# Decay products of an RWKV-7 block from its first token: inverse taken token-major, k and b scaled in place and then turned

## The chip, the cores and the metric

One core of one Trainium2 chip. The metric is device time in microseconds (us) of one launch, the median of three runs. The engines are named as in the profile: PE (TensorE), DVE (VectorE), ACT (ScalarE), POOL (GpSimd), SP (the queue that issues most transfers).

## The reference

A recurrent attention block is followed by a feed-forward layer. Batch 4, 8 heads, 768 tokens, 40 features a head; then 3072 rows of 320 go through 320 x 2048 and 2048 x 320 with a hard-swish between.

```python
# r, k, v, w, a, b: (4, 8, 768, 40); state: (4, 8, 40, 40)
for t in range(S):
    y[:, :, t] = einsum('bhd,bhde->bhe', rt, state)
    Sa = einsum('bhde,bhe->bhd', state, at)
    state = state * wt[:, :, None, :] - einsum('bhd,bhe->bhde', Sa, bt) \
            + einsum('bhd,bhe->bhde', vt, kt)
x = y.transpose(0, 2, 1, 3).reshape(3072, 320)
h = x @ w_in
out = (h * clip(h + 3.0, 0.0, 6.0) / 6.0) @ w_out
```

w lies between 0.85 and 0.95, and the two weight matrices arrive as 64-bit floats.

## The kernel before

The recurrence is cut into 24 **units**: unit i holds 64 tokens of 8 heads of two batch rows, so 128 rows of 320 values. Each group of 4 units covers the same 64 or the next 64 tokens of all four batch rows. Gamma is the running product of w inside a unit; a, k, b and the result are scaled by gamma or by its inverse, so that the recurrence over 64 tokens becomes matrix products and the inverse of a triangular 64 x 64 matrix for each head (called "inversion" below: a long series of small DVE operations for 4 units together, `prod` and `x` in the profile).

"Turning" is PE's transpose of a tile from token-major (tokens on partitions) to feature-major (features of two heads on partitions):

```python
def turn_pairs(x):                      # 4 transposes of 128 x 128 into one PSUM bank
    o = ps_any([P, NPR, P])             # five banks "any", used in turn
    for n in range(NPR):
        nc.tensor.transpose(out=o[:, n, :], in_=x[:, 2 * n:2 * n + 2, :]..., identity=ident[:])
    return o
```

The preparation of a unit counts gamma from the *middle* of the 64 tokens, backwards and forwards:

```python
def w_stage():
    wt = turn_pairs(o["WN"]); yield PE
    nc.scalar.activation(out=wv[:, :, 0, 1:HB + 1], in_=x[:, :, 0, ::-1], func=AF.Copy)
    nc.scalar.activation(out=wv[:, :, 1, 1:HB + 1], in_=x[:, :, 1, :], func=AF.Copy)
    fetch("W", following(i))
    nc.vector.tensor_tensor_scan(out=prods..., data0=wm[:], data1=start[:], ...)   # 128 x 528
def gam_stage():
    nc.vector.reciprocal(gv[:, :, 0:HB], prods backward half)                      # 128 x 256
    nc.gpsimd.tensor_copy(gv[:, :, HB:BL], ...)
    nc.gpsimd.tensor_copy(rv[:, :, 0:HB], ...)
    nc.gpsimd.tensor_copy(dec..., ...)            # the decay over each half unit
def a_stage():
    x = turn_pairs(o["AN"]); yield PE
    nc.vector.reciprocal(rv[:, :, HB:BL], prods forward half)                      # 128 x 256
    nc.vector.tensor_tensor(out=at[:], in0=x[:], in1=o["G"][:], op=ALU.mult)
def b_stage():                                    # k_stage is the same with K, kt
    x = turn_pairs(o["BN"]); yield PE
    nc.vector.tensor_tensor(out=bt[:], in0=x[:], in1=o["rg"][:], op=ALU.mult)
def factor_stage():                               # token-major k and b, needed later by sn and y
    (4 transposes of o["rg"]); yield PE
    nc.scalar.activation(out=rgt[:], in_=..., func=AF.Copy)
    t = grp.tile([P, HD + WPAD], F32, name="KBt", tag="KBt", bufs=NU + 2)
    nc.gpsimd.memset(t[:, 2 * HD:], 0.0)
    for name in "KB": nc.gpsimd.tensor_tensor(out=o[name]..., in0=o[name + "N"]..., in1=rgt[:], op=ALU.mult)
    for name in "BK": fetch(name, following(i))
```

F (at with bt) and E (at with kt) are matrix products of the scaled tiles. F feeds the inversion.

In a unit's own steps the state is scaled at the start and added to later, and the result is scaled at the end:

```python
def s_RT():
    ...
    nc.gpsimd.tensor_tensor(out=scale[:], in0=last_dec[p][:], in1=dec[:, 0], op=ALU.mult)
    nc.gpsimd.tensor_copy(last_dec[p][:], dec[:, 1])
    nc.vector.tensor_tensor(out=st..., in0=st..., in1=scale..., op=ALU.mult)
def s_sn():
    (64 matrix products of K, B with V, U); yield PE
    for q in range(2): nc.vector.tensor_tensor(out=st[:, q, :, 0:D], in0=sn[q], in1=st[:, q, :, 0:D], op=ALU.add)
def s_y():
    ...
    nc.gpsimd.tensor_tensor(out=yg[:], in0=m["ys"]..., in1=o["G"][:], op=ALU.mult)
```

The order of work is fixed in the program. At the start, the 64-bit weights are converted piece by piece (20 pieces, five steps each, lines 299 to 328) beside the preparation of the first group. A second group of four is prepared beside the weights' end. From unit 4 on the kernel is in its **steady part**: each unit takes four steps. In each step PE gets the attention products due in it first (those of the unit itself, and the preparation of a unit five ahead), and then about 3.5 pieces of the feed-forward layer, 6.2 while an inversion runs. Results are collected in a fixed order.

```python
OWN_STAGES   = [["RT", "VT"], ["R", "C", "S"], ["U", "UT", "rS"], ["sn", "H"], ["y"], ["move", "move2"]]
AHEAD_STAGES = [["W", "gam"], ["A", "B"], ["F", "K"], ["E", "factor"], ["EV"]]
CLOSE_STAGES = [["W", "gam"], ["A", "B"], ["F", "K", "factor"], ["E"], ["EV"]]
PRODUCTS = ["RT", "VT", "W", "S", "A", "B", "K", "factor", "y", "EV", "R", "C", "U", "UT", "rS", "sn", "H", "E", "F"]
RESULTS  = ["RT", "y", "W", "gam", "VT", "EV", "R", "S", "C", "A", "B", "move", "move2", "U", "UT", "rS", "F", "K", "sn", "H", "E", "factor"]
```

PRODUCTS is PE's order inside one part of a step, RESULTS that of the operations that empty PE's banks.

Of the kernel before, what the change touches and what calls it, by code (L numbers as in the profile page):

```python
# [8 lines left out]
F32 = mybir.dt.float32  # L9
# [20 lines left out]
def kernel(  # L30
# [52 lines left out]
    WPAD = HD + SLOT - D  # L83
# [74 lines left out]
    def second(name):  # L158

        tag = {"B": "S", "K": "U"}[name]  # L160
        return padded(grp.tile([P, H, SLOT], F32, name=name + "1", tag=tag, bufs=1), name)

# [8 lines left out]
    SCAN = NB * 2 * (HB + 1)  # L171
    start = const.tile([P, SCAN], F32, name="start")
    nc.vector.memset(start[:], 0.0)
    nc.vector.memset(start[:].rearrange("p (n i) -> p n i", i=HB + 1)[:, :, 0:1], 1.0)
    wm = const.tile([P, SCAN], F32, name="wm")
    nc.vector.memset(wm[:], 0.0)
    inputs, others = {}, {}
    for name in "WABK":
        inputs[name] = padded(const.tile([P, H, SLOT], F32, name=name), name)
    seconds()  # L180
    for name in "BK":
        others[name] = second(name)
# [17 lines left out]
    state, last_dec = [], []  # L200
    for p in range(NP):
        t = const.tile([P, 2, NPR, SLOT], F32, name=f"state{p}")
        nc.vector.memset(t[:], 0.0)
        state.append(t)
        t = const.tile([P, 2, NPR], F32, name=f"last{p}")
        nc.vector.memset(t[:], 1.0)
        last_dec.append(t)
# [47 lines left out]
    def load_weights():  # L255
# [24 lines left out]

        while load():
            pass
# [4 lines left out]
        parts = [grp.tile([P, HD + WPAD], F32, name=f"parts{n}", tag="KBt", bufs=NU + 2)  # L287
                 for n in range(2)]
        parts = [t[:, 0:2 * WC].bitcast(U32).rearrange("p (n c) -> p n c", n=2) for t in parts]
        for n in range(PIECES + 1):  # L290
            now = None
            if n < PIECES:
# [3 lines left out]
                hi = raw[:, :, :, 1]  # L296
                x = parts[n % 2]
                now = out, raw, x
# [5 lines left out]
            if before:  # L304
                out, raw, y = before
                m, yf = raw[:, :, :, 1].bitcast(F32), y.bitcast(F32)
# [3 lines left out]
                if len(out.shape) == 4:  # L310
                    m, yf = (z.rearrange("p n (j c) -> p n j c", c=out.shape[3]) for z in (m, yf))
                nc.vector.tensor_tensor(out=out, in0=m, in1=yf, op=ALU.mult)
# [6 lines left out]
            if now:  # L319
                nc.vector.scalar_tensor_tensor(x, hi, 0x80000000, x, ALU.bitwise_and,  # L320
                                               ALU.bitwise_or)
# [64 lines left out]
    def fetch(name, i, engine=None):  # L386
# [5 lines left out]
        if name == "V":  # L392
            t = values[i % AHEAD]
        else:
            t = (others if i < 2 * NU and i % 2 and name != "R" else inputs)[name]
# [55 lines left out]
    def prepare(i, F):  # L451
        n, o = i % NU, data[i]
        def w_stage():
            wt = turn_pairs(o["WN"])
            yield PE

            wv = wm[:].rearrange("p (r m i) -> p r m i", m=2, i=HB + 1)
            x = wt[:].rearrange("p r (q m i) -> p (r q) m i", q=2, m=2)
            nc.scalar.activation(out=wv[:, :, 0, 1:HB + 1], in_=x[:, :, 0, ::-1], func=AF.Copy)
            nc.scalar.activation(out=wv[:, :, 1, 1:HB + 1], in_=x[:, :, 1, :], func=AF.Copy)  # L460
            fetch("W", following(i))
            prods = o["prods"] = tmp.tile([P, NB, 2, HB + 1], F32, name="prods", bufs=2)
            nc.vector.tensor_tensor_scan(  # L463
                out=prods[:].rearrange("p r m i -> p (r m i)"), data0=wm[:], data1=start[:],
                initial=0.0, op0=ALU.mult, op1=ALU.add,
            )

        def gam_stage():

            gam = o["G"] = grp.tile([P, NPR, P], F32, name="gam", tag="gam", bufs=NU + 2)  # L470
            rgam = o["rg"] = tmp.tile([P, NPR, P], F32, name="rgam", bufs=2)
            gv = gam[:].rearrange("p r (q i) -> p (r q) i", q=2)
            rv = rgam[:].rearrange("p r (q i) -> p (r q) i", q=2)
            nc.vector.reciprocal(gv[:, :, 0:HB], o["prods"][:, :, 0, 1:HB + 1][:, :, ::-1])  # L474
            nc.gpsimd.tensor_copy(gv[:, :, HB:BL], o["prods"][:, :, 1, 0:HB])
            nc.gpsimd.tensor_copy(rv[:, :, 0:HB], o["prods"][:, :, 0, 0:HB][:, :, ::-1])
            dec = grp.tile([P, 2, 2, NPR], F32, name="dec", tag="dec", bufs=NU + 2)
            nc.gpsimd.tensor_copy(dec[:].rearrange("p m q r -> p r q m"),
                                  o["prods"][:].rearrange("p (r q) m i -> p r q m i", q=2)[:, :, :, :, HB])
            o["dec"] = dec  # L480
            if i <= 2 * NU:
# [3 lines left out]
        def a_stage():  # L485
            x = turn_pairs(o["AN"])
            yield PE
            rv = o["rg"][:].rearrange("p r (q i) -> p (r q) i", q=2)
            nc.vector.reciprocal(rv[:, :, HB:BL], o["prods"][:, :, 1, 1:HB + 1])  # L489
            at = o["at"] = grp.tile([P, NPR, P], F32, name="at", tag="at")  # L490
            nc.vector.tensor_tensor(out=at[:], in0=x[:], in1=o["G"][:], op=ALU.mult)
            fetch("A", following(i))

        def b_stage():
            x = turn_pairs(o["BN"])
            yield PE
            bt = o["bt"] = turned("bt")
            nc.vector.tensor_tensor(out=bt[:], in0=x[:], in1=o["rg"][:], op=ALU.mult)
# [42 lines left out]
        def factor_stage():  # L541

            rg = ps_any([P, NPR, P])
            for pr in range(NPR):
                nc.tensor.transpose(out=rg[:, pr, :], in_=o["rg"][:, pr, :], identity=ident[:])
# [3 lines left out]
                out=rgt[:], in_=rg[:].rearrange("p r (s e) -> p (r s) e", s=2)[:, :, 0:D],  # L549
                func=AF.Copy,  # L550
            )
            t = grp.tile([P, HD + WPAD], F32, name="KBt", tag="KBt", bufs=NU + 2)
            nc.gpsimd.memset(t[:, 2 * HD:], 0.0)
            for x, name in enumerate("KB"):
                o[name] = t[:, x * HD:x * HD + WPAD]
                nc.gpsimd.tensor_tensor(  # L556
                    out=o[name][:, 0:HD].rearrange("p (h e) -> p h e", h=H),
                    in0=o[name + "N"][:, :, 0:D], in1=rgt[:], op=ALU.mult,
                )
            if i > 2 * NU:  # L560
                fetch("V", i)
            for name in "BK":
                fetch(name, following(i))

        def k_stage():
            x = turn_pairs(o["KN"])
            yield PE
            kt = o["kt"] = turned("kt")
            nc.vector.tensor_tensor(out=kt[:], in0=x[:], in1=o["rg"][:], op=ALU.mult)
# [6 lines left out]
        def ev_stage():  # L576
# [10 lines left out]
            for q in range(2):  # L587
# [4 lines left out]
        return {"W": w_stage, "gam": gam_stage, "A": a_stage, "B": b_stage, "F": f_by_32 if i < 2 * NU else f_by_64,  # L592
                "factor": factor_stage, "K": k_stage, "E": e_stage, "EV": ev_stage}

    def in_turn(stages, order):

        for name in order:
            yield from stages[name]()
# [3 lines left out]
    def by_stages(i, stages):  # L602


        order = ["K", "factor", "F"] if i % NU < 2 else ["K", "F", "factor"]
        return in_turn(stages, ["W", "gam", "A", "B"] + order + ["E", "EV"])
# [85 lines left out]
    def step(i):  # L692
# [3 lines left out]
        st, dec, VN = state[p], o["dec"], o["VN"]  # L696
# [3 lines left out]
        def s_RT():  # L700
# [5 lines left out]
            if fresh:  # L706
                nc.gpsimd.tensor_copy(last_dec[p][:], dec[:, 1])
                return
# [583 lines left out]
```

## Time and profile before

| what | value |
|---|---|
| time, median of three | 855.09 us (852.67 to 856.62) |
| span of the profiled execution | 853.2 us |
| PE busy | 774.1 us, 91% |
| DVE busy | 529.4 us, 62% |
| ACT busy | 310.1 us, 36% |
| POOL busy | 157.5 us, 18% |
| matrix products of the feed-forward layer (lines 921, 926, 945) | 197.6 + 55.8 + 234.8 us of PE time |
| chain of work that ended last | PE 78%, DVE 12% |

The busy share is an average over parts of the run with different limits. The table of the span in equal stretches says more than the sum: it shows PE idle for long only in about the first 200 us. In a program with a fixed order on each engine, a row of the timeline says when an instruction started, how long it took, and in brackets what it waited for; a row without brackets had not waited.

### The profile page before, as it was taken

What the parts mean: (1) busy time and instruction counts of PE and PEld (TensorE: products, weight loads), DVE (VectorE), ACT (ScalarE), POOL (GpSimd) and SP (SyncE); (2) the same over time, 40 slices, a digit from 0 to 9 for tenths busy, and PEclk for the clock granted to TensorE, in tenths of its full rate; (3) what the DMA queues carried; (4) which work ended last, traced back from release to release, by engine and by line L of the source; (5) the groups of instructions that cost most, each with busy time, mean ns of one, the idle gap of its engine ahead of it and who ended that gap; (6) DMA issues with size and microseconds to landing.
All of it is one profiled execution on the core that took longest, in us unless ns stands there. A gap on an engine that the chain in (4) does not pass through costs nothing.

```text
span 853.2 us, 34881 instructions
## 1 busy us (share of the span) xinstructions
PE 774.1 (91%) x15480; PEld 660.0 (77%) x15480; DVE 529.4 (62%) x1032; ACT 310.1 (36%) x756; POOL 157.5 (18%) x307
## 2 busy tenths in 40 slices
PE   4723877898999989999999999999999999999998
PEld 3622766776888878888888888888888888888886
DVE  6988598878864579734698454697445674221211
ACT  1322654231344433444324534334453324222111
POOL 3231212112121130221211122113012202000000
PEclk9755878899999999999999999999999999999999
DMA  7572443331123330322231232222232101110000
GB/s 137 86 181 80 112 113 80 64 57 24 33 49 67 59 62 11 61 50 46 46 56 29 43 66 49 45 42 39 41 55 50 18 20 27 25 22 12 17 18 15
DMA packets 174213, 44.99 MB, mean 53 GB/s; under 512 B 157424, under 2 KB 172784, under 8 KB 174064
## 3 DMA queue, kind: packets, MB, share of 16 engines
q1 hardware_dynamic: 171920, 42.44, 26.0%
q8 instruction: 122, 2.00, 1.0%
q10 hardware_dynamic: 2144, 0.33, 0.2%
q14 instruction: 27, 0.22, 0.1%
HBM read 34.08 MB, written 3.93 MB: 45 GB/s over the span
## 4 chain that ended last, share of the span: by engine, by line
PE 78%; DVE 12%; issue 3%; ACT 2%; POOL 1%; DMA 1%; SPq 0%; DVEq 0%; ACTq 0%
PE o L945 24%; PE h L921 20%; PE any L420 6%; PE h L926 5%; PE any L438 3%; PE any L841 3%; PE any L818 3%; DVE prod L626 2%; PE any L660 2%; PE any L679 2%; DVE x L632 2%; PE any L763 2%; PE any L784 1%; PE any L725 1%; PE any L583 1%
## 5 line engine op out<-in xcount | busy, mean ns | idle before, releaser
L945 PE MATMUL o<-wout,gt 128*128 128x320 f32 x768 | 234.8, 449 | 0.0
L921 PE MATMUL h<-xt,win 128*128 128x128 f32 x1536 | 197.6, 283 | 3.2 <-DVE gt L932 3.2
L921 PEld LDWEIGHTS h<-xt,win 128*128 128x128 f32 x1536 | 186.4, 196 | 12.1 <-DVE gt L932 3.9
L945 PEld LDWEIGHTS o<-wout,gt 128*128 128x128 f32 x768 | 139.2, 191 | 54.3 <-issue 1.2
L932 DVE SCALAR_TENSOR_TENSOR gt<-gt,h 128x512 f32<-128x512 f32 x96 | 61.4, 681 | 95.4 <-ACT gt L931 95.4
L931 ACT ACTIVATE gt<-h,three 128x512 f32<-128x512 f32 x96 | 60.8, 684 | 128.0 <-PE h L926 127.8
L856 POOL TENSOR_TENSOR yg<-ys,gam 128x512 f32<-128x512 f32 x24 | 41.3, 1723 | 212.5 <-DVE ys L853 153.9
L626 DVE TENSOR_TENSOR prod<-x 128x30 f32<-128x30 f32 (+9 forms) x180 | 64.1, 356 | 13.4 <-POOL x L617 8.1
L632 DVE TENSOR_TENSOR x<-x,prod 128x30 f32<-128x30 f32 (+9 forms) x180 | 63.9, 355 | 5.5 <-DVE prod L626 0.3
L556 POOL TENSOR_TENSOR KBt<-K,rgt 128x320 f32<-128x320 f32 x24 | 21.6, 899 | 221.6 <-ACT rgt L548 216.3
L926 PE MATMUL h<-xt,win 64*128 64x128 f32 x768 | 55.8, 285 | 0.0
L447 DVE COPY_PREDICATED score<-mask,any 128x256 f32<-128x256 int32 x143 | 53.2, 434 | 1.1 <-PE any L438 1.1
L926 PEld LDWEIGHTS h<-xt,win 64*128 64x128 f32 x768 | 46.6, 187 | 5.2 <-issue 0.3
L474 DVE RECIPROCAL gam<-prods 128x256 f32<-128x256 f32 x24 | 41.5, 1741 | 13.4 <-POOL yg L856 13.1
L825 DVE TENSOR_TENSOR state<-any,state 128x160 f32<-128x160 f32 x48 | 13.3, 319 | 56.0 <-PE any L438 54.5
L489 DVE RECIPROCAL rgam<-prods 128x256 f32<-128x256 f32 x24 | 41.8, 1741 | 0.0
L589 ACT ACTIVATE EV<-any 64x160 f32<-64x160 f32 x92 | 24.8, 295 | 44.4 <-PE any L583 32.6
L463 DVE TENSOR_TENSOR_SCAN prods<-wm,start 128x528 f32<-128x528 f32 x24 | 30.1, 1253 | 16.6 <-ACT wm L460 15.0
L853 DVE TENSOR_TENSOR ys<-any,ys 128x256 f32<-128x256 f32 x44 | 16.6, 418 | 34.5 <-PE any L583 19.9
L704 ACT ACTIVATE RT<-any 128x512 f32<-128x512 f32 x24 | 14.3, 595 | 59.4 <-PE any L420 59.4
L841 PE MATMUL any<-score,KBt 64*64 64x64 f32 x1536 | 31.4, 230 | 2.7 <-DVE score L447 1.6
L841 PEld LDWEIGHTS any<-score,KBt 64*64 64x64 f32 x1536 | 27.3, 142 | 7.6 <-issue 3.3
(184 smaller groups left out, 1137.7 us busy)
## 6 DMA issues: line engine op xcount, KB each, us to landing
B<-in_b_dram SPq DMA_DIRECT2D x48, 80.0 KB
K<-in_k_dram SPq DMA_DIRECT2D x48, 80.0 KB
V<-in_v_dram SPq DMA_DIRECT2D x96, 40.0 KB
out_dram<-ob SPq DMA_DIRECT2D x48, 80.0 KB
R<-in_r_dram SPq DMA_DIRECT2D x92, 40.0 KB
W<-in_w_dram SPq DMA_DIRECT2D x40, 80.0 KB
A<-in_a_dram SPq DMA_DIRECT2D x40, 80.0 KB
xt<-yg SPq DMA_DIRECT2D x72, 40.0 KB
```

The source lines that it names most:

```text
L420: nc.tensor.transpose(out=o[:, n, :], in_=x[:, 2 * n:2 * n + 2, :].rearrange("p s e -> p (s e)"), identity=ident[:])
L447: nc.vector.copy_predicated(out=x[:, 4 * i:4 * i + 4, :], mask=mask4, data=o[i])
L474: nc.vector.reciprocal(gv[:, :, 0:HB], o["prods"][:, :, 0, 1:HB + 1][:, :, ::-1])
L489: nc.vector.reciprocal(rv[:, :, HB:BL], o["prods"][:, :, 1, 1:HB + 1])
L626: nc.vector.tensor_tensor(out=pv, in0=_ap(x[:], (i + 1) * L + i, [[L, n], [0, i]]), in1=_ap(x[:], i * L, [[0, n], [1, i]]), op=ALU.mult,)
L632: nc.vector.tensor_tensor(out=rest, in0=rest, in1=pv, op=ALU.add)
L841: nc.tensor.matmul(out=y[q][half(s), pr, :], lhsT=o[name][half(q), h * D:h * D + SLOT], rhs=m[name][half(q), 4 * rs + 2 * s + j, :], start ...
L921: nc.tensor.matmul(out=hp[c][:, i, :], lhsT=win[:, t, j * P:(j + 1) * P], rhs=xt[:, t, :], start=(t == 0 and i == 0), stop=False)
L926: nc.tensor.matmul(out=hp[c][:, i, :], lhsT=win2[half(c), (j0 + i) * P:(j0 + i + 1) * P], rhs=xt[half(c), 2, :], start=False, stop=(i == N ...
L931: nc.scalar.activation(out=gt[:], in_=hp[c][:], func=AF.Relu, bias=three[:], scale=1.0)
L932: nc.vector.scalar_tensor_tensor(out=gt[:], in0=gt[:], scalar=6.0, in1=hp[c][:], op0=ALU.min, op1=ALU.mult)
L945: nc.tensor.matmul(out=op[:], lhsT=gts[c][:, n, :], rhs=wout[:, c * HJ + r * NQ + n, :], start=((split or r == 0) and c == 0 and n == 0), ...
```

## The change

Gamma is counted from the unit's first token. Then it is at most 1, the scan writes it directly, its inverse is needed only where k and b are scaled, and the decay of the whole unit is its last column. Only one reciprocal is left, taken in the token-major form (128 x 320 without the padding). k and b are scaled once, in place, token-major, and then turned, so that feature-major k and b need no multiplication but only a copy out of PSUM, given to ACT. The aim is less work on DVE. Buffers for k and b become seven (`scaled`), so that the loaded tile can be kept as the scaled one. The decay of the state moves to the end of a unit, on POOL in the steady part. The order of stages is set anew.

```diff
+            nc.scalar.activation(out=wm[:, :, 1:BL], in_=x[:, :, 1:BL], func=AF.Copy)
+            nc.scalar.activation(out=start[:, :, 0], in_=x[:, :, 0], func=AF.Copy)
             fetch("W", following(i))
+        def scan():
+            gam = o["G"] = grp.tile([P, NB, BL], F32, name="gam", tag="gam", bufs=NU + 2)
             nc.vector.tensor_tensor_scan(out=gam..., data0=wm..., data1=start..., ...)      # 128 x 512
-        def gam_stage():       (one reciprocal 128 x 256 on DVE, three copies on POOL)
         def a_stage():
-            nc.vector.reciprocal(rv[:, :, HB:BL], o["prods"][:, :, 1, 1:HB + 1])
+            nc.vector.tensor_tensor(out=y[:, :, 1:BL], in0=x[:, :, 1:BL], in1=o["G"][:, :, 0:BL - 1], op=ALU.mult)
+            nc.scalar.activation(out=y[:, :, 0], in_=x[:, :, 0], func=AF.Copy)
+        def turn_scaled(name, to):                 # b_stage and k_stage
+            x = turn_pairs(o[name])
+            yield PE
+            t = o[to] = turned(to)
+            nc.scalar.activation(out=t[:], in_=x[:], func=AF.Copy)
-        def factor_stage():
+        def g_stage():
             (4 transposes, now of gamma) ... rgt copied by ACT
+            nc.vector.reciprocal(rgt[:], rgt[:])                                            # 128 x 320
+            for name in "BK":
+                t = o[name] = o[name + "N"]
+                nc.gpsimd.tensor_tensor(out=t[:, :, 0:D], in0=t[:, :, 0:D], in1=rgt[:], op=ALU.mult)
 ...
         def s_RT():
-            nc.gpsimd.tensor_tensor(out=scale[:], ...); nc.gpsimd.tensor_copy(last_dec[p][:], dec[:, 1])
-            nc.vector.tensor_tensor(out=st[:, :, :, 0:D], in0=st[:, :, :, 0:D], in1=scale..., op=ALU.mult)
         def s_sn():
+            if i + NP < NK:
+                (nc.vector if i < NU else nc.gpsimd).tensor_tensor(out=st..., in0=st..., in1=o["dec"], op=ALU.mult)
         def s_y():
+            nc.gpsimd.tensor_tensor(out=x[:, :, 1:BL], in0=y[:, :, 1:BL], in1=o["G"][:, :, 0:BL - 1], op=ALU.mult)
+            nc.gpsimd.tensor_copy(x[:, :, 0], y[:, :, 0])
 ...
-    TWOS = 14                # first and second group: W, gam, A, B, K, factor, F, E, EV by pairs
+    TWOS = ["0", "0", "0", "1", "10", "0", "10", "0", "01", "1", "1", "1", "1"]
+    # each pair of units: "W scan", "A", "G", "B", "F", "K", "E", "EV"
-    AHEAD_STAGES = [["W", "gam"], ["A", "B"], ["F", "K"], ["E", "factor"], ["EV"]]
+    AHEAD_STAGES = [["W", "scan"], ["A", "G"], ["B", "K", "F"], ["E", "V"], ["EV"]]
+    PRODUCTS = ["RT", "VT", "W", "S", "A", "G", "B", "K", "y", "EV", "R", "C", "U", "UT", "rS", "sn", "H", "E", "F"]
+    RESULTS  = ["RT", "y", "W", "VT", "EV", "R", "S", "C", "A", "G", "B", "K", "U", "UT", "rS", "F", "sn", "H", "E", "scan", "V", "move", "move2"]
+                if banks + need > 5 or name == "F" and any(x == "B" for x, _ in begun):
                     finish()
```

Beside this, the converted weights keep their intermediate in the place of the result instead of in a buffer of their own.

## The prediction

> **What bounds the kernel now.** I first read the busy table of six stretches of the span, chosen where the character of the run changes. Columns: stretch, its length, busy time (instructions) of PE, its weight loads, DVE, ACT, POOL, then PE's clock, the DMA share, GB/s.
>
> ```profile
> 0.00:80.00 80.00, 33.09 (x672) 28.23 (x672) 69.78 (x135) 21.82 (x54) 20.68 (x55) 0.72 0.63 129
> 80.00:140.00 60.00, 44.32 (x1241) 40.11 (x1242) 45.91 (x90) 32.40 (x72) 14.35 (x29) 0.76 0.40 99
> 140.00:215.00 75.00, 67.01 (x1067) 55.28 (x1067) 61.62 (x104) 20.00 (x53) 15.69 (x29) 0.93 0.29 51
> 215.00:340.00 125.00, 120.78 (x2529) 102.83 (x2526) 86.41 (x169) 51.88 (x135) 23.71 (x49) 0.99 0.26 46
> 340.00:840.00 500.00, 499.78 (x9947) 427.51 (x9948) 264.34 (x537) 182.27 (x441) 83.03 (x145) 1.00 0.21 38
> ```
>
> PE is idle 46.9, 15.7, 8.0, 4.2 and 0.2 us in these, and 4.1 us in the end. From 215 us on it is full: there only PE's own work and new waits of PE count, and work taken from DVE is worth nothing by itself. PE's work doesn't change: six turns and one transpose of gamma or its inverse in a unit before and after, the same products. So the question is how much of the 70.6 us of idle time in the first 215 us goes away, and whether new waits come up later.
>
> Next the groups by line, for the durations (busy us, mean ns | idle before).
>
> ```profile
> L489 DVE RECIPROCAL rgam<-prods 128x256 f32<-128x256 f32 x24 | 41.8, 1741 | 0.0
> L556 POOL TENSOR_TENSOR KBt<-B,rgt 128x320 f32<-128x320 f32 x24 | 20.9, 873 | 0.0
> L569 DVE TENSOR_TENSOR kt<-any,rgam 128x512 f32<-128x512 f32 x24 | 16.2, 686 | 10.1 <-PE any L420 10.1
> L736 ACT ACTIVATE VT<-any 128x512 f32<-128x512 f32 x24 | 14.4, 602 | 0.0
> L712 DVE TENSOR_TENSOR state<-state,scale 128x320 f32<-128x320 f32 x22 | 10.6, 483 | 6.6 <-POOL scale L710 6.6
> ```
>
> Then the timelines at two places of the start.
>
> ```profile
> 47.24 0.43 DVE L299 TENSOR_SCALAR parts<-raw 128x512 uint32<-128x512 uint32 x1 [0.41 <-DMA raw<-in_moe_w_in_dram]
> 101.00 0.49 DVE L712 TENSOR_TENSOR state<-state,scale 128x320 f32<-128x320 f32 x1 [3.92 <-POOL scale L710]
> ```
>
> The first is the third weight piece: DVE waits for its transfer already now. The second is DVE held for 3.92 us by a small POOL operation, which goes away.
>
> **What the Trainium skill says.** (1) VectorE: DVE Perf Modes, on the 8-slice pipeline, says that the reciprocal is an iterative divide on repeated ALU passes, hence several cycles an element; under its errata heading a fp32 two-input operation takes (N+151)/0.96 ns. For N = 512 that is 691 ns, the trace has 686. The trace's 1741 ns agree with an expensive element: with the same 157 ns of fixed cost, (1741-157)/256 = 6.2 ns each. (2) ScalarE: Activation LUTs, on what ACT_TABLE_LOAD costs, gives 186 + 0.833 N ns for an ACTIVATE with immediates: 613 ns at 512, against 602 in the trace. (3) GPSIMD Engine Reference, section 3.1, gives about 2.6 cycles an element for two inputs, against 1 on DVE; the trace agrees in kind (873 ns for 320 elements on POOL, 483 on DVE). (4) PSUM — Partial Sum Buffer, on engine and sequencer instructions, says that matrix products start and complete in program order. So feed-forward products behind a turn that waits cannot overtake it. The trace has no counterexample.
>
> **The change, part by part, for one unit.**
>
> - Off DVE: two reciprocals, 2 x 1.74; the multiplications of bt and kt, 0.68 + 0.69; the state's, 0.48 (from unit 4 on). On DVE: one reciprocal of 320 elements, estimated 0.157 + 320 x 0.0062 = 2.14. The scan loses 16 of 528 elements, 0.04. Sum: 5.37 - 2.14 = 3.2 us a unit, some 75 us in all; DVE ends near 455 us.
> - On ACT: the copies of bt and kt, 2 x 0.60; the copy of w as 504 + 8 elements instead of twice 256, about 0.0; one more small copy of 8 elements, 0.2. Sum 1.4 us a unit, 34 in all; ACT ends near 344 us, 40%.
> - POOL: three copies, two small operations of the decay and a memset go (0.44 + 0.43 + 0.24 + 0.27 + 0.21 + 0.12 = 1.7 us by their rows); the state's multiplication (0.88) and a small copy (0.24) come. POOL loses 0.6 us a unit, some 15.
>
> **First 80 us: nearly nothing.** DVE has 4 x 3.2 = 13 us less to do before the first inversion, less some for units 0 and 1. But SP issues its transfers one by one, about 0.66 us each (the V rows: 8 in 5.26), and is busy without a break from 0.8 us. The third weight piece has 54 issues ahead of it before, and 58 after, since k and b of unit 4 are now fetched ahead of it: 0.8 + 58 x 0.66 = 39 us plus the pauses that remain, against 40.59 now. It landed at 47.14, 6.5 us later. The program puts DVE's step on this piece at the inversion's third small operation, where before six were done. So I expect DVE to reach the inversion early and then to stand until 46 to 47. Gain: 0.5 us.
>
> **80 to 140 us.** The wait of 3.92 us goes, and units 0 to 3 now have four state multiplications on DVE where there were two (1 us more). Gain: 3 us.
>
> **140 to 215 us.** The second group's preparation takes 13 us from a DVE that is 82% busy, but PE can gain no more than its 8.0 us of idle time. The new chain there, gamma turned, reciprocal, POOL, then B turned, has to run inside the same program. I take half: 4 us.
>
> **215 to 340 us.** One wait of PE for a DVE score (3.2 us at 317 us) lies behind a held-up reciprocal. I take 1.5 us of it.
>
> **The steady part: a new wait.** G stands in one step and B in the next. Between them DVE has R, the scores of C, at, and then the reciprocal; then POOL scales b, then k; only then can PE turn them. Today bt is made in the first of these steps on DVE, and nothing of PE waits. The timelines of DVE and PE for one unit:
>
> ```profile
> 532.28 0.56 DVE L730 TENSOR_TENSOR RR<-any,EV 128x160 f32<-128x160 f32 x2 [0.84 <-PE any L438]
> 532.75 0.77 DVE L447 COPY_PREDICATED score<-mask,any 128x256 f32<-128x256 int32 x2
> 533.41 1.74 DVE L489 RECIPROCAL rgam<-prods 128x256 f32<-128x256 f32 x1
> 535.08 0.63 DVE L491 TENSOR_TENSOR at<-any,gam 128x512 f32<-128x512 f32 x1
> 529.66 0.60 PE L747 MATMUL any<-ident,state 128*128 128x128 f32 x4
> 535.49 0.60 PE L420 MATMUL any<-ident,K 128*128 128x128 f32 x4
> ```
>
> After the change DVE is free for at at 533.41. Then at 0.55 (start to start), the reciprocal 2.14, b on POOL 0.87, two hand-overs of 0.05: b is ready 3.66 us later, at 537.07, and k 0.82 later. PE wants b at 535.49, so it stands 1.58 us; the turn of b takes 0.43, and k is waited for 0.39 more. Sum 2.0 us, at every unit like this one. The same sum for the units prepared in the steady part (start of L489, start of the K turn, both from the two timelines): 1.0 for the first; then 0, 0.3, 1.1, 0.45, 0.64, 1.15, 2.0, 0.3, 0.64, 1.15, 2.0 for the eleven from 346 us on. Sum 10.7. For the three in between, F follows directly on the turns and waits for ACT's copy, about 0.4 each: 1.2. Together 11.9 us; I count 11, since a few gt operations ahead of R may start earlier on a lighter DVE.
>
> **Sum.** 855.1 - 0.5 - 3 - 4 - 1.5 + 11 = 857. Since the order was visibly set anew for this change, and the start holds more idle time than I dare to count on, I move this a little to the better: **854 us**.
>
> **The rivals.** (A) The relief of DVE counts in full at the start: 9 us of the 15.7 between 80 and 140 and 6 of 8 after, and the steady waits are small because DVE gets to R sooner. For it: DVE is 77 to 87% busy in the first 215 us. Against: the transfer that ends DVE's wait at 47 us, and products in the steady part that PE, not DVE, releases. It would give 840. (B) The steady waits as above with no gain at the start, because B of the second group also waits for POOL: 865. (C) ACT becomes the bound of the third of the four steps: F's eight copies take 2.6 us, U, UT and ys about 2.1, and bt and kt 1.2 more, in a step of about 7 us; gt comes late and PE waits for it. Against: 4.5 us of PE work lie between an expand and the reuse of its banks, and PE waited for gt in all of the steady part for 0.2 us. It would add up to 8 us to (B).
>
> **Range and chances.** The gains could be 4 to 20 us, the new waits 4 to 16, mostly independent, so some 11 us either way: **843 to 866**. Two per cent are 17 us. Faster by that needs (A) almost in full: **0.10**. Slower by that needs (B) and (C): **0.06**. Within 2%: **0.84**.
>
> **What would show it.** Right: DVE near 455 us and ACT near 344; a group of reciprocals of 128x320 near 2.1 us; DVE waiting for the third weight piece for several us near 40 to 47; in PE's waits, the turn of b or k waiting for POOL, some 10 us in total, in the steady part. Wrong: a PE that is still full from 340 us on (then the G-to-B chain fits, and the time is under 850), or a start in which PE is full well before 200 us (then DVE alone was its bound), or waits of PE for gt or for PSUM banks that ACT empties.

## The result, and the profile after

The changed kernel takes 891.45 us (median; 888.03 to 896.28) against 855.86 us of the kernel before: a ratio of 1.0418, interval 1.037 to 1.0466. It is slower by 4.2%, outside the predicted range of 843 to 866. The profiled execution has a span of 894.6 us against 853.2, so there are 41.4 us to find; the medians lie 35.6 apart, since the profiled execution of the changed kernel is the slowest of its four (896.28).

The busy table of the same six stretches of the changed kernel (same columns as in the prediction):

```profile
0.00:80.00 80.00, 35.21 (x672) 29.55 (x672) 51.54 (x105) 26.61 (x66) 19.27 (x47) 0.65 0.67 122
80.00:140.00 60.00, 38.13 (x1069) 34.62 (x1070) 45.49 (x95) 29.47 (x65) 12.15 (x26) 0.70 0.40 99
140.00:215.00 75.00, 63.23 (x1150) 53.89 (x1149) 47.61 (x84) 27.11 (x69) 12.09 (x14) 0.86 0.29 54
215.00:340.00 125.00, 115.00 (x2170) 96.31 (x2173) 61.23 (x122) 50.67 (x126) 17.50 (x25) 0.96 0.26 45
340.00:840.00 500.00, 488.38 (x9973) 415.27 (x9966) 244.45 (x522) 196.95 (x489) 70.20 (x101) 0.99 0.20 38
```

DVE has 18 us less in the first 80 us, 14 us less in the third stretch, 25 in the fourth. PE used none of it: from 80 us on it is less busy in every stretch, and its clock is lower in every stretch. The fifth, which was full (0.2 us idle), has 11.6 us idle.

The groups by line, for the pieces of the change (busy us, mean ns, then the idle time before them):

```profile
L553 DVE RECIPROCAL rgt<-rgt 128x320 f32<-128x320 f32 x24 | 51.2, 2146 | 22.3 <-ACT rgt L549 22.3
L556 POOL TENSOR_TENSOR KB<-KB,rgt 128x320 f32<-128x320 f32 x48 | 42.5, 907 | 193.8 <-DVE rgt L553 193.8
L419 PE MATMUL any<-ident,KB 128*128 128x128 f32 x184 | 30.6, 300 | 15.7 <-POOL KB L556 15.7
L419 PEld LDWEIGHTS any<-ident,KB 128*128 128x128 f32 x184 | 22.4, 151 | 24.6 <-POOL KB L556 23.2
L492 ACT ACTIVATE bt<-any 128x512 f32<-128x512 f32 x24 | 14.2, 595 | 40.5 <-PE any L419 40.5
```

The durations are those that the prediction worked with. The third and fourth lines are the new wait: the turn of k and b stands for POOL, 15.7 us at the products and 23.2 us at their weight loads (the two overlap).

To cut the 41.4 us, take the start of each group's inversion as a mark. It begins with the only transpose `fb<-F` on DVE; `tb<-x` is the end of it.

| stretch | before | after | difference | predicted |
|---|---|---|---|---|
| 0 to end of the first inversion | 78.58 | 84.75 | +6.2 | -0.5 |
| to the second inversion (189.26; 199.03) | 110.68 | 114.28 | +3.6 | -7 (-3 and -4) |
| to the third (302.36; 326.33) | 113.10 | 127.30 | +14.2 | -1.5 |
| to the end (853.2; 894.6) | 550.84 | 568.27 | +17.4 | +11 |

The predicted stretches were cut at round times, so the columns match only roughly. A second way to cut: the time in which PE stands, and the time it loses by a lower granted clock (its busy time times one minus the clock, summed over slices of about 4 us). The first goes from 79.2 to 104.7 us, the second from 27.3 to 41.0; that is 25.5 + 13.7 = 39.2 of the 41.4 us. The 13.7 belong to this pair of executions: the mean granted clock is 0.927 in the profiled one of the changed kernel and 0.933 to 0.939 in its three others; before it is 0.948, where 63 other executions of that kernel lie between 0.933 and 0.952, 0.942 on average. Between two middling executions the clock's part is smaller.

Where PE stands, from its timeline after the change (start, duration, and in brackets the idle time before it with what ended it). The start of the run:

```profile
20.60 1.28 SPq L405 DMA_DIRECT2D A<-in_a_dram  x2
26.82 1.08 PE L419 MATMUL any<-ident,A 128*128 128x128 f32 x4 [7.67 <-DMA A<-in_a_dram]
```

PE reaches the turn of `a` of the third unit at 19.2 us and stands for its transfer. The turn of gamma of the same unit, its inverse, and b and k of all four units need no `a`, but they come after it in PE's order. The same turn in the kernel before:

```profile
28.52 1.12 PE L420 MATMUL h<-ident,A 128*128 128x128 f32 x4
```

It did not wait, although SP issued its transfer at 22.00 us, 1.4 us later than now, and behind eight transfers of V as now. Turns and products of the first two units lay ahead of it in PE's order, from 16.6 us on. So the transfer of `a` is not later; its turn has moved ahead of work that does not need it. Behind this place PE stands once more, for ScalarE's copy of `kt`:

```profile
38.34 0.36 PE L437 MATMUL h<-at,kt 40*64 40x64 f32 x1 [4.04 <-ACT kt L492]
36.76 0.72 ACT L297 ACTIVATE win<-win,low 128x512 uint32<-128x512 uint32 x1 [2.50 <-DVE win L295]
37.70 0.59 ACT L492 ACTIVATE kt<-any 128x512 f32<-128x512 f32 x1
```

k was turned by 34.3 us, but in ScalarE's order a step of the weights came first, and that stood for DVE. Near 310 us:

```profile
309.28 0.28 PE L572 MATMUL any<-V,score 64*64 64x40 f32 x2 [3.51 <-DMA V<-in_v_dram]
```

Here the product of a score with V waits for V itself (5.8 us in five waits). And in the steady part, one unit on DVE, POOL and PE, the same kind of place that the prediction showed at 532 us:

```profile
631.55 0.76 DVE L446 COPY_PREDICATED score<-mask,any 128x256 f32<-128x256 int32 x2
632.21 0.68 DVE L483 TENSOR_TENSOR at<-any,gam 128x504 f32<-128x504 f32 x1
633.52 2.15 DVE L553 RECIPROCAL rgt<-rgt 128x320 f32<-128x320 f32 x1 [0.63 <-ACT rgt L549]
...
636.66 0.66 PE L419 MATMUL any<-ident,KB 128*128 128x128 f32 x4 [1.02 <-POOL KB L556]
637.48 0.66 PE L419 MATMUL any<-ident,KB 128*128 128x128 f32 x4 [0.16 <-POOL KB L556]
```

The chain is the predicted one: scores, at, inverse, POOL, turn. The inverse stands last of the three on DVE. The state's decay, which stood 3.92 us for POOL at 101 us before, now follows on DVE without a wait of its own (DVE stands 3.19 us for PE's products just ahead of it):

```profile
96.63 0.49 DVE L808 TENSOR_TENSOR state<-state,gam 128x320 f32<-128x320 f32 x1
```

### The profile page after: what moved, and what is told of

The parts are those of the page before. It is cut to its first block, busy times and chain, and to the rows that moved or that the text cites. A ratio compares the mean times of both kernels' runs of the same rounds, so it can differ in the third digit from the quotient of the medians.

```text
span 894.6 us, 34679 instructions
## 1 busy us (share of the span) xinstructions
PE 789.9 (88%) x15480; PEld 669.9 (75%) x15480; DVE 458.7 (51%) x941; ACT 338.5 (38%) x828; POOL 132.6 (15%) x215
## 4 chain that ended last, share of the span: by engine, by line
PE 65%; DVE 13%; SPq 6%; issue 6%; POOL 3%; DMA 3%; ACT 3%; ACTq 0%; POOLq 0%; DVEq 0%
PE o L930 20%; PE h L906 16%; PE any L419 5%; PE h L911 4%; PE any L437 3%; PE any L798 3%; PE any L824 3%; DVE rgt L553 2%; POOL KB L556 2%; SPq L405 2%; SPq L402 2%; DVE prod L614 2%; DVE x L620 2%; PE any L743 2%; PE any L648 2%
## 5 line engine op out<-in xcount | busy, mean ns | idle before, releaser
L556 POOL TENSOR_TENSOR KB<-KB,rgt 128x320 f32<-128x320 f32 x48 | 42.5, 907 | 193.8 <-DVE rgt L553 193.8
L614 DVE TENSOR_TENSOR prod<-x 128x30 f32<-128x30 f32 (+9 forms) x180 | 61.2, 340 | 13.5 <-POOL x L605 8.1
L553 DVE RECIPROCAL rgt<-rgt 128x320 f32<-128x320 f32 x24 | 51.2, 2146 | 22.3 <-ACT rgt L549 22.3
L840 POOL TENSOR_TENSOR yg<-ys,gam 128x504 f32<-128x504 f32 x24 | 30.5, 1270 | 192.5 <-DVE ys L836 74.3
L419 PE MATMUL any<-ident,KB 128*128 128x128 f32 x184 | 30.6, 300 | 15.7 <-POOL KB L556 15.7
L462 DVE TENSOR_TENSOR_SCAN gam<-wm,start 128x512 f32<-128x512 f32 x24 | 29.4, 1223 | 29.4 <-POOL yg L840 18.2
L419 PEld LDWEIGHTS any<-ident,KB 128*128 128x128 f32 x184 | 22.4, 151 | 24.6 <-POOL KB L556 23.2
L808 POOL TENSOR_TENSOR state<-state,gam 128x320 f32<-128x320 f32 x18 | 13.3, 738 | 181.3 <-DVE state L805 181.3
L836 DVE TENSOR_TENSOR ys<-any,ys 128x256 f32<-128x256 f32 x44 | 16.7, 420 | 42.1 <-PE any L572 25.5
L710 DVE TENSOR_TENSOR RR<-any,EV 128x160 f32<-128x160 f32 x44 | 12.2, 319 | 48.0 <-PE any L437 48.0
L602 DVE STREAM_TRANSPOSE fb<-F 128x1024 f32<-128x1024 f32 x6 | 12.9, 2158 | 43.7 <-ACT F L537 30.0
```

The lines of the kernel that those rows point to most:

```text
L553: nc.vector.reciprocal(rgt[:], rgt[:])
L556: nc.gpsimd.tensor_tensor(out=t[:, :, 0:D], in0=t[:, :, 0:D], in1=rgt[:], op=ALU.mult)
L614: nc.vector.tensor_tensor(out=pv, in0=_ap(x[:], (i + 1) * L + i, [[L, n], [0, i]]), in1=_ap(x[:], i * L, [[0, n], [1, i]]), op=ALU.mult,)
L840: nc.gpsimd.tensor_tensor(out=x[:, :, 1:BL], in0=y[:, :, 1:BL], in1=o["G"][:, :, 0:BL - 1], op=ALU.mult)
```

## The experiments

The theory: three separate causes, all in the order of things and none in the amount of work. (1) The inverse stands last in its step on DVE. (2) V of units 9 to 11 is fetched a step later than before. (3) In the start PE stands at the turn of `a`. A fourth came up when these were undone. The rival: the work itself has moved to engines that are now the bound (ScalarE, rival C of the prediction; or POOL), in which case an undone order brings little.

**V early.** The list of stages for the units that follow closely on one another, which the change took out, is put back in the new kernel's terms.

```diff
+    CLOSE_STAGES = [["W", "scan"], ["A", "G"], ["B", "K", "F", "V"], ["E"], ["EV"]]
-            ahead[u, m] = prepared(u), AHEAD_STAGES
+            close = coming and begins[coming[0]] < m + BLOCKS
+            ahead[u, m] = prepared(u), CLOSE_STAGES if close else AHEAD_STAGES
```

> The changed kernel with one thing put back: for units 8 to 11, V is fetched one step earlier (with B, K, F instead of with E), as the kernel before did. Theory (several separate waits of PE, each with a slower clock behind it): the 5.8 us that PE waits for V's transfer in EV vanish, and with them most of the 5 us that the clock loses between 199 and 326 us; 881 to 886 us in place of 891. Rival (ACT with its copies of bt and kt is the new bound, the V waits are only where it shows): 889 to 892, PE waits elsewhere instead. Second rival (all of the loss is the relation of reciprocal, POOL and the turn of b): 890.

Measured: 881.23 us, ratio to before 1.0316 (1.0292 to 1.034); 10.2 us come back. The third inversion begins at 313.9 instead of 326.3. In the stretch up to it PE's idle time falls from 10.8 to 4.6 us and the clock's loss from 6.6 to 1.6 us. So V's later fetch cost 10 us through one place of some 5 us of waiting, and about half of it was the slower clock behind that place.

**Gamma first.** In the order in which results of a step are taken, the inverse goes ahead of R, the state's copy, C and at.

```diff
-    RESULTS = ["RT", "y", "W", "VT", "EV", "R", "S", "C", "A", "G", "B", "K",
+    RESULTS = ["RT", "y", "W", "VT", "EV", "G", "R", "S", "C", "A", "B", "K",
```

> The changed kernel with one word moved in the order of results: G ahead of R, S, C and A, so that DVE takes the reciprocal first in its step instead of after R, the scores and at. Theory (PE waits for POOL's b and k because the reciprocal stands last on DVE): the 15.7 us that PE waits at the turns of k and b fall below 4, 876 to 882 us in place of 891. Rival (POOL itself is too slow or too late): the waits stay above 10 us, 888 or more. Second rival (ACT's copies): no change, 889 to 892.

Measured: 872.77 us, ratio 1.0212 (1.0192 to 1.0231); 18.7 us come back, more than expected. The same group as above, of this kernel:

```profile
L419 PE MATMUL any<-ident,KB 128*128 128x128 f32 x184 | 27.9, 296 | 3.7 <-POOL KB L556 3.7
L419 PEld LDWEIGHTS any<-ident,KB 128*128 128x128 f32 x184 | 23.8, 153 | 7.0 <-POOL KB L556 3.9
```

The products' wait falls by 12.0 us and the weight loads' by 19.3. The time that came back is near the second number: some of the standing lies inside what the profile counts as busy time of PE, which is 7.8 us less from the third inversion on, 3.4 of them by the clock. POOL's work is unchanged, 48 multiplications of 0.9 us; so POOL was late and not too slow.

**B first.** In the start, the turn of b of the first pair of units goes ahead of the turns of `a` of the second pair, and later b of the second pair ahead of EV of the first.

```diff
-    TWOS = ["0", "0", "0", "1", "10", "0", "10", "0", "01", "1", "1", "1", "1"]
+    TWOS = ["0", "0", "0", "1", "01", "0", "10", "0", "10", "1", "1", "1", "1"]
```

> The changed kernel with the order in two places of the first and second group turned round: B of the first pair ahead of A of the second pair, and B of the second pair ahead of EV of the first. Theory (at the start PE stands 7.7 us at the turn of A of unit 2, whose transfer is late, and B of units 0 and 1 waits behind it in PE's order; later B of units 2 and 3 waits behind EV): the first inversion starts near 42 us in place of 49, ends near 79 in place of 84.8, total 882 to 887 us. Rival (the third weight piece limits the inversion anyway, as the prediction had it): it starts earlier and waits for the piece, the end stays within 2 us of 84.8, 889 to 892.

Measured: 888.69 us, ratio 1.0403 (1.0378 to 1.0427); 2.8 us come back by the medians, which the spread of the runs (888.03 to 892.11 against 888.03 to 896.28) does not tell from nothing; in the profile the inversion begins at 45.9 and ends at 81.7, 3.1 us sooner. Less than expected: PE still stands 5.9 us for the same transfer of `a`, with less behind it.

**All three.**

> All three edits together. Theory (separate waits that add up, 36 us of which these are about 29): 858 to 868 us. Rival (one shared bound, ACT or POOL, behind all of them): no better than the best single one by more than 4 us, 875 or more.

Measured: 864.57 us, ratio 1.0112 (1.0091 to 1.0133); of the 31.7 us of the three by themselves 26.9 remain together, and the intervals leave room for the full sum. From the third inversion on this kernel is level with the one before (550.0 us against 550.8), and after 340 us PE waits for 0.2 us in all. What is left lies ahead of it: 3.5 us up to the end of the first inversion, 5.4 us from there to the second, 1.2 us to the third. In the second of these stretches, POOL and then PE:

```profile
168.78 1.25 POOL L840 TENSOR_TENSOR yg<-ys,gam 128x504 f32<-128x504 f32 x1 [27.12 <-DMA xt<-yg]
...
171.06 4.23 POOL L556 TENSOR_TENSOR KB<-KB,rgt 128x320 f32<-128x320 f32 x4
```

```profile
171.97 0.66 PE L419 MATMUL any<-ident,KB 128*128 128x128 f32 x4 [3.87 <-POOL KB L556]
174.53 1.12 PE L419 MATMUL any<-ident,KB 128*128 128x128 f32 x4 [0.86 <-POOL KB L556]
```

POOL stands for the transfer that empties the buffer of a scaled result, and k and b stand behind that in POOL's order. In the kernel before, feature-major b came from DVE, and PE's turn of b waited for nothing of POOL.

**A first.** All three, and V of the first four units is fetched behind `a` instead of ahead of it.

```diff
-            if i <= 2 * NU:
+            if NU <= i <= 2 * NU:
                 fetch("V", i)
     ...
             fetch("A", following(i))
+            if i < NU:
+                fetch("V", i)
```

> The three undone parts together, and V of the first four units fetched behind their A instead of ahead of it. If the first 82 us are set by the tensor engine standing in order at the turn of A of the third unit (5.9 to 7.7 us behind A's transfer), A2 lands about 3 to 5 us sooner and the first inversion begins near 43 and ends near 79: 859 to 862 in all. If the vector engine's own work sets it, as the prediction had it, A's earlier landing changes nothing: 864 to 865, inversion again at 46 to 82.

Measured: 863.2 us, ratio 1.009 (1.0064 to 1.0117). PE's wait for `a` falls from 6.5 to 3.7 us (2.8 for the third unit, 0.9 for the fourth), and the inversion begins at 42.5 but ends only at 80.2: 3.8 us sooner at its begin, 1.8 at its end, 1.4 in the whole, which is inside the spread of the runs. The median lies between the two expectations. The wait was there, but little stood behind it.

**k and b on DVE in the second group.** All three, and:

```diff
-                nc.gpsimd.tensor_tensor(out=t[:, :, 0:D], in0=t[:, :, 0:D], in1=rgt[:], op=ALU.mult)
+                (nc.vector if NU <= i < 2 * NU else nc.gpsimd).tensor_tensor(
+                    out=t[:, :, 0:D], in0=t[:, :, 0:D], in1=rgt[:], op=ALU.mult)
```

> The three undone parts together, and for the units of the second group the multiplication of k and b on the vector engine instead of GpSimd. If the second group loses its time because GpSimd, in order, stands behind the moved rows and k and b stand behind it, the wait of the tensor engine at the turn of b and k falls from 4.7 us to under 1 us and the second inversion begins 4 to 6 us sooner (192 to 194 instead of 198): 857 to 861. If the late transfers of that group are the cause and GpSimd only shows them, the turn waits for another thing and the time stays at 863 to 866.

Measured: 861.11 us, ratio 1.0069 (1.0044 to 1.0094). The second inversion begins at 193.8 instead of 198.2, and the turns no longer wait for the scaled k and b:

```profile
169.15 0.63 PE L419 MATMUL any<-ident,KB 128*128 128x128 f32 x4
172.10 0.63 PE L419 MATMUL any<-ident,KB 128*128 128x128 f32 x4 [1.43 <-issue]
```

So this fourth cause is shown: eight operations taken off an engine that was 15% busy were worth 3.5 us, because of what they stood behind.

**The start as a whole.** All three, V behind `a`, k and b on DVE for the first eight units, and the raw weights a little earlier (`limit[0] = {5: 4, ...}` and `t == 5` for 7).

> Both changes of the start and of the second group together (V behind A for the first four units; k and b multiplied on the vector engine for the first eight), and the raw third and fourth weight pieces fetched a little earlier. If the two causes are separate and add up, the first inversion begins near 43, the second near 190: 850 to 856, level with the kernel before. If the start is limited by the vector engine, the eight multiplications added to it there take back what they give: 861 to 866.

Measured: 858.72 us, ratio 1.0039 (1.0023 to 1.0054). The second inversion begins at 190.15, 0.9 us behind the kernel before. The two causes add up, but the whole stays a little slower than before, 2.7 us above the expected top.

**Gamma turned ahead of `a`.** On top of the start version, in the first four units: b and k are fetched ahead of `a`, V behind b's turn, one entry of the pair order is as in the changed kernel again (`"10"` for the first `"01"`), and:

```diff
-        return in_turn(stages, ["W scan", "A", "G", "B", "F", "K", "E", "EV"])
+        first = ["G", "A"] if i < NU else ["A", "G"]
+        return in_turn(stages, ["W scan"] + first + ["B", "F", "K", "E", "EV"])
```

> As the combined start version (k and b of the first eight units multiplied on the vector engine, raw weights a little earlier), with gamma turned ahead of a in the first four units, b and k fetched ahead of a, and V fetched after b's turn. If the start is late because everything behind A's turn has to wait for A in the tensor engine's order although gamma, its reciprocal, b and k do not need A, then the first inversion begins 4 to 8 us sooner than 43.8 (36 to 40) and ends at 73 to 77: 850 to 855, at or under the kernel before. If a bound behind it takes over (the weight pieces that the vector engine converts inside the inversion), the inversion begins early but still ends near 80: 857 to 860.

Measured: 858.94 us, ratio 1.0036 (1.0019 to 1.0054). The inversion begins at 41.9 and ends at 77.65, 0.9 us sooner than in the kernel before. That gain is then lost: the second begins at 193.0. The waits of PE for gamma's scan are new (4.6 us in all); what remains at the turns of `a` is 4.3 us. The time lies where the second expectation had it, but both failed in the profile: the inversion neither began at 36 to 40 nor ended near 80.

**The same for the second group**, with k and b on DVE for the first twelve units (`i < 2 * NU` and `i < 3 * NU` in the two edits):

> As the run above, with gamma ahead of a in the second group too and k and b multiplied on the vector engine for the first twelve units. If order is the whole loss, the second inversion comes another 1 to 3 us sooner and the stretch up to the third takes 80.5 us instead of 82.6: 847 to 853. If the second group is limited by the transfers on the one queue, moving b and k ahead of a only exchanges one wait for another: within 2 us of the run above.

Measured: 857.56 us, ratio 1.0034 (1.0021 to 1.0048). The second inversion begins at 190.0, but the stretch from its end to the third is 83.6 us, not 80.5. Within 2 us of the run above; none of these orders is faster than the kernel before.

**The copies on DVE instead of ScalarE**, in the changed kernel, nothing else:

```diff
-            nc.scalar.activation(out=t[:], in_=x[:], func=AF.Copy)
+            nc.vector.tensor_copy(t[:], x[:])
```

> The changed kernel with the two copies of the turned b and k (48 of 0.60 us) done by the vector engine instead of ScalarE, nothing else. If ScalarE's added work is a cause of the loss (rival C), 4 us or more come back: under 887. If it is not, ScalarE was not the bound: 889 to 894.

Measured: 920.81 us, ratio 1.0758 (1.0716 to 1.08): 29 us slower than the changed kernel, which neither side expected. PE and DVE of this kernel near 355 us:

```profile
352.67 0.66 PE L419 MATMUL any<-ident,KB 128*128 128x128 f32 x4 [0.87 <-POOL KB L556]
...
362.08 1.02 PE L780 MATMUL any<-RT,S 40*64 40x64 f32 x27 [6.59 <-DVE bt L492]
```

```profile
361.05 0.38 DVE L620 TENSOR_TENSOR x<-x,prod 128x210 f32<-128x210 f32 x1
361.34 0.68 DVE L492 COPY bt<-any 128x512 f32<-128x512 f32 x1
```

b is turned by 353.3 and copied only at 361.34, behind a row of the inversion's small operations. Until then the PSUM bank is held, and another product of PE waits for this copy. Whether ScalarE's copies cost the changed kernel anything is answered by the waits of its PE after 340 us (in all, times, longest):

```profile
PE any L419 <- POOL KB L556: 10.9, 20, 2.2
PE any L526 <- issue: 0.6, 1, 0.6
```

ScalarE does not stand in this list, which settles rival (C) for the steady part. It does not settle it for the start: in the first 100 us PE waits 9.3 us for ScalarE's copies of `kt` in the changed kernel, 8.5 in the start as a whole and 4.9 with gamma first in both groups, against 3.1 us for DVE's bt and kt in the kernel before. The run by itself only shows that DVE is no place for the copies; with them there the same waits in the start are 10.5 us.

**The kernel before with late V**, the reverse of the first experiment:

```diff
-    CLOSE_STAGES = [["W", "gam"], ["A", "B"], ["F", "K", "factor"], ["E"], ["EV"]]
+    CLOSE_STAGES = AHEAD_STAGES
```

> The kernel before with one thing of the change done to it alone: the units prepared in the three close stages get their V one step later, by the same list of stages as all others. If the late V costs what it cost in the changed kernel (10 us when undone there), the time goes to 862 to 867. If V only waits because the changed kernel is late in other things there, it stays at 855 to 858.

Measured: 859.96 us, ratio 1.0058 (1.0041 to 1.0076): 5.0 us slower, between the two. In its profile the stretch from the end of the second inversion to the third is 88.9 us instead of 80.3, but PE waits there for b, not for V (2.83 us here, 2.79 us at 295.86):

```profile
272.90 0.63 PE L420 MATMUL any<-ident,B 128*128 128x128 f32 x4 [2.83 <-DMA B<-in_b_dram]
```

The one queue passes the delay on to whatever stands next in it. That the list of stages costs time in this place is confirmed; that it does so through V is shown only in the changed kernel.

**The kernel before with a lighter DVE.** The last question is what the relief of DVE could have brought at all. Of the first eight units the two reciprocals are replaced by copies on ScalarE, which is loaded more by them; the run leaves out the inverse of the running product there, and only its time is of use.

```diff
+        def inverse(i, out, in_):
+            if i < 2 * NU:
+                nc.scalar.activation(out=out, in_=in_, func=AF.Copy)
+            else:
+                nc.vector.reciprocal(out, in_)
-            nc.vector.reciprocal(gv[:, :, 0:HB], o["prods"][:, :, 0, 1:HB + 1][:, :, ::-1])
+            inverse(i, gv[:, :, 0:HB], o["prods"][:, :, 0, 1:HB + 1][:, :, ::-1])
-            nc.vector.reciprocal(rv[:, :, HB:BL], o["prods"][:, :, 1, 1:HB + 1])
+            inverse(i, rv[:, :, HB:BL], o["prods"][:, :, 1, 1:HB + 1])
```

> The kernel before, with the sixteen reciprocals of its first eight units left out: ScalarE copies the products in their place (about 0.4 us each), so the output is not the reference's, and the vector engine is 16 times 1.74 = 28 us lighter in the first 190 us, with no other chain, transfer or order changed. If the relief of the vector engine is what the start could have gained from (rival A), the first inversion begins 3 to 5 us sooner than 40.1, the second 9 to 15 us sooner than 189.3: 840 to 847. If the chains of transfers and hand-overs set the start and the vector engine's share only fills it, the first begins within 2 us and the second within 4 us of before: 851 to 856.

Measured: 851.23 us, ratio 0.9952 (0.9929 to 0.9974). The inversions begin at 38.9 and 183.2 instead of 40.1 and 189.3. DVE in the first 40 us of this kernel, and just ahead of the inversion:

```profile
0.00:40.00 40.00, 24.58 (x521) 21.68 (x525) 21.99 (x37) 14.26 (x40) 12.93 (x44) 0.87 0.66 114
```

```profile
31.95 0.69 DVE L504 TENSOR_TENSOR bt<-h,rgam 128x512 f32<-128x512 f32 x1 [2.20 <-PE h L420]
38.89 2.16 DVE L620 STREAM_TRANSPOSE fb<-F 128x1024 f32<-128x1024 f32 x1 [0.45 <-ACT F L524]
```

DVE is busy for 22.0 us of the 40 instead of 32.7, and the inversion comes 1.2 us sooner: DVE now stands for PE's turns (2.20 us here, 2.18 at 34.82). 28 us off DVE are worth 4.2 us of time, 15%, and they arrive around the second inversion. The time is as the second expectation had it; the second inversion moved further (6.0 us) than that one allowed.

## Why the prediction was wrong, point by point

**The sizes held.** DVE 455 us predicted, 458.7 measured; ACT 344, 338.5; the inverse of 128x320 2.14 us, 2.146. POOL alone lost more than counted: 24.9 us where some 15 were taken off.

**The steady wait: right in mechanism.** 11 us were summed from the timelines of before; PE's own wait for POOL at this turn after 340 us is 10.9 us, at 20 places. At 631 us it is 1.18 us for a unit, where the prediction had up to 2.0. What was too small is the price: 17.4 us of time from the third inversion on, and 18.7 came back when the inverse was put first. The weight loads stood for 17.5 us there, and the clock's loss is 3.4 us against 1.7. The prediction also chose to move the sum by 3 us "to the better", since the order "was visibly set anew for this change". The new order was itself the cause.

**The step that failed: the four terms of the start, "- 0.5 - 3 - 4 - 1.5".** They hold that a lighter DVE can only help up to 340 us, and look for new waits in the steady part alone. Measured: +6.2, +3.6, +14.2, or 24 us instead of -9. In detail:

- **First 80 us.** The prediction had DVE stand for the third weight piece at the inversion. It never did: it stood 5.9 us for F, which came late because PE had stood 7.7 us for `a` and 4.0 us for `kt` ahead of it. The prediction followed the queue of transfers to one transfer, and did not follow PE's own order there. The transfer of `a` came no later than before; its turn was put ahead of work that did not need it. In the version that turns gamma ahead of `a` the inversion ends at 77.65 us, 0.9 us sooner than before the change.
- **80 to 215 us.** The small wait of 3.92 us behind POOL did go, and more than its gain was lost. The prediction named the chain "gamma turned, reciprocal, POOL, then B turned" and assigned it half of PE's idle time as a gain. It did not ask what POOL is doing at that time: it stood 27 us for a transfer. That was rival (B), "B of the second group also waits for POOL"; it put the worst case at "no gain at the start", where a loss was due.
- **215 to 340 us.** The wait for V of units 9 to 11 was nowhere in the sum. The whole diff shows the list of stages for close units gone and V one step later; neither line was followed to PE. It cost 10.2 us.
- **What the relief is worth.** Up to 9 us were taken. The last experiment gives a size: 28 us off DVE in the first eight units bring 4.2 us.

**The clock was not in the prediction at all.** Its loss rises by 13.7 us between the two profiles, a third of their difference. The Trainium skill (TensorE: Matmul & The Clock Gate, part 1, the HAM clock gate) says that the gate lowers PE's clock after a window of about 3.4 us in which PE was idle. The trace agrees in kind. Behind the wait of 3.51 us for V, in the changed kernel (same columns as the busy table):

```profile
310.90:321.00 10.10, 9.79 (x133) 7.16 (x134) 3.39 (x5) 1.47 (x6) 2.42 (x3) 0.50 0.30 50
```

PE is busy for 9.79 of these 10.10 us, at half clock (0.50), while in the 19 us behind them the clock is 1.00 again. With V fetched early the clock's loss in the stretch up to the third inversion goes from 6.6 to 1.6 us. A wait of that length should have been priced with the slower time behind it.

**What stays open.** With all orders mended the kernel is still 0.34% (0.21 to 0.48) slower than before, although its DVE is lighter. PE's idle time up to the second inversion is about the same (66.1 us against 67.4); the clock's loss is 29.7 against 24.0, and 3 us are lost between the second inversion's end and the third begin. The start as a whole and the two versions with gamma first have nearly equal times, and their profiles differ in the clock's loss up to the first inversion from 0.5 to 9 us, so one profile does not tell whether that is a cause. No run took away PE's waits for ScalarE's copies of `kt` in the start by themselves. No order that was tried beats the kernel before, and whether one exists is not settled.

## What to carry to other kernels

When a change rebuilds the order of stages, follow each moved fetch and each new producer to the in-order engine behind it: price what that engine is doing at that time, not the size of the operation that moved. Relief of an engine that is not the bound is worth a fraction of its size (here 15%), while a wait put on the engine that is the bound cost its length here (18.7 us, for 12.0 of waiting products and 19.3 of waiting weight loads), and more where the clock fell behind it (10.2 us for V, of which 5.8 are waits). An engine that is 15% busy can still be the latest in a chain, if something ahead in its order waits for a transfer; and results that leave PSUM belong on an engine whose order has nothing long in it at that time.

## What was not expected of the hardware

- A wait of PE shows in the profile as two: at the products (10.9 us after 340 us) and at their weight loads (17.5 us for the same turns). The time that came back, 18.7 us, is nearer to the second.
- 48 copies of 0.68 us moved from ScalarE to DVE (0.60 us each there) cost 29 us, on an engine that was half idle. In the profiled executions 20.5 of 24.6 us lie behind the third inversion (588.8 us against 568.3): PE's idle time there is 13.2 us more, which the three waits for DVE's copies (6.59, 3.81 and 3.63 us, 14.0 together) account for, and the clock's loss about 6 us more.
